# Decode attention over a KV cache on one core: VectorE and ScalarE as loops over the pairs, q's projection as a loop over 8 groups of 4 heads

## The chip, the cores and the metric

The kernel runs on one core of a Trainium2 chip. The time is the device time of one execution in microseconds. The kernel before takes 662.87 us (median of 3 runs, 662.78 to 663.01). The profiled execution has a span of 660.4 us from its first to its last instruction. In the profile PE is TensorE's matmuls, PEld its weight loads, DVE is VectorE, ACT ScalarE, POOL GpSimd and SP the engine that issues DMA transfers.

## The reference

Two blocks share one layer-normalized input x (2 tokens of width 512), and their results are added to x:

```
xn = layernorm(x)                                  # (2, 1, 512)
q  = xn @ wq          -> 2 x 32 heads of 128        # wq (512, 4096)
s  = q . k_cache * 128**-0.5                        # k_cache (2, 32, 8192, 128)
o  = softmax(s) . v_cache                           # v_cache the same shape
a  = concat(o) @ wo                                 # wo (4096, 512)
f  = relu(xn @ w1) @ w2                             # w1 (512, 1792), w2 (1792, 512)
out = x + a + f
```

All tensors are bf16. The two caches are 2 x 134 MB; everything else together is some 12 MB. The work per cache element is tiny, one product with one query.

## The kernel before, in words

There are 64 combinations of token and head. They are worked on in NP = 32 pairs; one pair of K, and one of V, is a tile of 128 partitions by 16384 elements (4 MB): 64 partitions for each of the two heads, 128 keys in each partition. R = 2 buffers hold K (ks), two hold V (vs). The second V buffer first holds wq.

What each engine does in pair t:

- TensorE (function step, L269) first waits for K(t) and for q of the pair (sQ1, L273). Then, in NG = 16 groups of 8, it transposes K blocks into PSUM (transposes, L230, matmul at L233), and two groups later multiplies the copied block with q (scores, L236, matmul at L240). Then it does the weighted sum over V of the pair before (weighted, L250, matmul at L253), and in between transposes the column of maxima (L288) and broadcasts the maximum (L291). TensorE already runs this as a loop of 16 turns of two pairs (L297), with the pair's number in a register that its waits compare with.
- VectorE and ScalarE share the copies of the transposed groups from PSUM to SBUF (kcopy, L378 to L380): groups 0, 3, 5, 8, 11 and 13 are ScalarE's (ON_ACT), the other ten VectorE's. VectorE also takes the maxima (L425, L430). ScalarE copies the broadcast maximum (nm, L483), takes Exp (L487), and copies the weighted sum of the pair before from PSUM into OTf (out_copy, L470 to L473). Both are written out in full, pair after pair: `for t in range(NP)` at L416 and L476 is a loop of the program that builds the kernel.
- GpSimd copies q of each pair into a small buffer (q2, L203), two pairs ahead.
- SyncE issues the transfers in order (L155 to L171): wq, K0, K1 and V0 at once; then for each t a K tile as soon as the transposes of pair t have ended (pT, L162), and a V tile as soon as the weighted sum that used its buffer has ended (sW, L164); last x again, w1, w2 and wo in three parts.

Semaphores order all of it. pT counts the groups of transposes over all pairs; group e of pair t is the number 16 t + e + 1, and VectorE, ScalarE and SyncE wait for such numbers. sA tells ScalarE that its own small copies are done. sO tells TensorE that a weighted sum has been copied away.

Ahead of the pairs the layer norm is done on VectorE and ScalarE, and TensorE projects q: 32 heads times 4 parts of the width, 128 products of a 128x128 block of wq with the two tokens (L216 to L225), into one PSUM tile. VectorE scales the result into qb (L408), and GpSimd copies the first two pairs' columns (L203). After the pairs come the last weighted sum, the feed-forward block, and the projections with w2 and wo (L306 to L376).

## Time and profile before

| what | number |
|---|---|
| time, median of 3 | 662.87 us |
| span of the profiled execution | 660.4 us |
| TensorE matmuls, busy | 551.0 us (83%), 12864 instructions |
| VectorE, busy | 251.4 us (38%), 433 instructions |
| ScalarE, busy | 236.7 us (36%), 389 instructions |
| read from HBM | 280.50 MB, mean 425 GB/s |
| 4 MB transfers of K | 32, median 26.8 us from issue to landing |
| 4 MB transfers of V | 32, median 31.6 us from issue to landing |
| copies L380, VectorE | 320 of 691 ns |
| copies L380, ScalarE | 192 of 1012 ns |
| products of q's projection L218 | 128, 3.6 us busy |

Busy time is the time in which an engine worked on an instruction; matmuls are pipelined, so a busy TensorE is not one at its peak. The page also cuts the span into 40 slices of 16.5 us and gives for each engine a digit, the busy share in tenths. Its DMA row is the mean busy share of the 16 DMA engines. The time from issue to landing holds the time that a transfer waits behind others in the queue. A list by waits says who waited for whom, and a list in order of time says when an instruction started and how long it took. Beside the page the trace has a record of each DMA packet, of each completion of a transfer by each of the 16 engines, and of the instructions that only the sequencers work on (register operations, branches, waits), which the page doesn't count as busy.

### The profile page before, as it was taken

Reading aid. Unit: us, or ns where it says so; the run is one execution under the profiler, and the core shown is the slowest. Engines: PE = TensorE matmul, PEld = TensorE weight load, DVE = VectorE, ACT = ScalarE, POOL = GpSimd, SP = SyncE. Lnnn points to the kernel's source line nnn. Section 1 sums busy time; section 2 is a strip of 40 time slices with the busy share of each in tenths; the row PEclk is TensorE's granted clock in tenths of the full one; section 3 lists DMA queues with packets and bytes.
Section 4 is the critical chain, followed back from the end, with each engine's and each line's share of the span. In section 5 each row is a group of like instructions: output and inputs, shape, how many; then the busy total and the mean of one; then the engine's idle time right before and its main releaser. Section 6 shows DMA issues by size and latency. Waiting matters only on the chain.

```text
span 660.4 us, 26876 instructions
## 1 busy us (share of the span) xinstructions
PE 551.0 (83%) x12864; PEld 537.0 (81%) x12864; DVE 251.4 (38%) x433; ACT 236.7 (36%) x389; POOL 8.5 (1%) x44
## 2 busy tenths in 40 slices
PE   2577999898887889788798987887997878987976
PEld 2577999888887889788798887887987878987875
DVE  1233544344343434434344443343443433443411
ACT  1242444343433334333243343333343333343410
POOL 1000000000000000000000000000000000000000
PEclk9999999998898999889899898899898989997985
DMA  9999999999999999999999999999999999999995
GB/s 381 416 438 429 424 439 427 437 427 431 437 429 437 427 431 433 429 437 429 431 435 427 439 429 431 435 427 439 427 431 433 429 439 425 435 433 429 437 417 246
DMA packets 10133, 280.73 MB, mean 425 GB/s; under 512 B 1154, under 2 KB 1156, under 8 KB 1284
## 3 DMA queue, kind: packets, MB, share of 16 engines
q1 hardware_dynamic: 10112, 280.50, 98.9%
q8 instruction: 10, 0.16, 0.1%
q14 instruction: 7, 0.06, 0.0%
q10 hardware_dynamic: 4, 0.00, 0.0%
HBM read 280.50 MB, written 0.00 MB: 425 GB/s over the span
## 4 chain that ended last, share of the span: by engine, by line
DMA 62%; PE 34%; ACT 1%; issue 1%; SPq 0%; DVE 0%
DMA ks<-in_A_k_cache_dram 56%; PE tp L233 21%; PE Sc L240 10%; DMA wo_sb<-in_A_wo_dram 5%; PE ot L253 3%; ACT kT L380 1%; PE ot L356 0%; PE Sc L288 0%; PE Sc L291 0%; SPq L171 0%; SPq L168 0%; SPq L166 0%; SPq L149 0%; SPq L167 0%; SPq L147 0%
## 5 line engine op out<-in xcount | busy, mean ns | idle before, releaser
L233 PE MATMUL tp<-identb,ks 128*128 128x128 bf16 x4096 | 324.9, 229 | 77.8 <-DMA ks<-in_A_k_cache_dram 75.9
L380 DVE COPY kT<-tp 128x1024 bf16<-128x1024 bf16 x320 | 219.7, 691 | 332.9 <-PE tp L233 332.7
L233 PEld LDWEIGHTS tp<-identb,ks 128*128 128x128 bf16 x4096 | 256.1, 103 | 81.3 <-DMA ks<-in_A_k_cache_dram 79.1
L380 ACT COPY kT<-tp 128x1024 bf16<-128x1024 bf16 x192 | 194.3, 1012 | 249.6 <-PE tp L233 249.6
L240 PE MATMUL Sc<-q,kT 128*128 128x64 bf16 x4096 | 216.3, 196 | 3.4 <-ACT kT L380 3.4
L240 PEld LDWEIGHTS Sc<-q,kT 128*128 128x128 bf16 x4096 | 178.4, 100 | 6.7 <-ACT kT L380 6.7
L253 PE MATMUL ot<-prm,vs 128*128 128x64 bf16 x4224 | 157.6, 193 | 8.5 <-issue 5.0
L253 PEld LDWEIGHTS ot<-prm,vs 128*128 128x128 bf16 x4224 | 140.5, 98 | 11.4 <-issue 8.8
L483 ACT COPY nm<-Sc 128x2 f32<-128x2 f32 x32 | 5.1, 160 | 118.2 <-PE Sc L291 118.2
L487 ACT ACTIVATE prm<-Sc,nm 64x128 bf16<-64x128 f32 x64 | 25.8, 402 | 1.4
L425 DVE TENSOR_REDUCE mcol<-Sc 64x1 bf16<-64x128 f32 x64 | 18.6, 291 | 17.6 <-PE Sc L240 17.2
L473 ACT COPY OTf<-ot 128x2 f32<-128x2 f32 x33 | 5.3, 160 | 35.3 <-PE ot L253 35.3
L430 DVE TENSOR_REDUCE mx<-Sc 1x2 bf16<-1x128 bf16 x32 | 8.9, 279 | 16.9 <-PE Sc L288 16.9
L203 POOL COPY q<-qb 128x2 bf16<-128x2 bf16 x32 | 5.8, 184 | 582.3 <-PE Sc L240 568.6
L487 ACT ACTIVATION_READ_ACCUMULATOR prm<-Sc,nm 64x1 f32 x64 | 11.8, 185 | 0.0
L218 PE MATMUL ot<-xnT,vs 128*128 128x2 bf16 x128 | 3.6, 165 | 8.3 <-DMA vs<-in_A_wq_dram 8.3
L218 PEld LDWEIGHTS ot<-xnT,vs 128*128 128x128 bf16 x128 | 3.5, 104 | 8.4 <-issue 8.4
L288 PE MATMUL Sc<-identb,mcol 128*1 128x128 bf16 x32 | 7.0, 217 | 0.0
L356 PE MATMUL ot<-OX,wo_sb 128*128 128x2 bf16 x128 | 3.7, 166 | 3.1 <-DMA wo_sb<-in_A_wo_dram 3.1
L356 PEld LDWEIGHTS ot<-OX,wo_sb 128*128 128x128 bf16 x128 | 3.6, 104 | 3.3 <-DMA wo_sb<-in_A_wo_dram 1.9
L291 PE MATMUL Sc<-mx,onesb 1*128 1x2 bf16 x32 | 5.5, 172 | 0.0
L436 DVE CAST xT<-tp 128x8 f32<-128x8 bf16 x1 | 0.2, 166 | 12.5 <-PE Sc L327 12.5
(49 smaller groups left out, 29.4 us busy)
## 6 DMA issues: line engine op xcount, KB each, us to landing
ks<-in_A_k_cache_dram SPq DMA_DIRECT2D x32, 4096.0 KB, 26.8
vs<-in_A_v_cache_dram SPq DMA_DIRECT2D x32, 4096.0 KB, 31.6
vs<-in_A_wq_dram SPq DMA_DIRECT2D x1, 4096.0 KB, 12.2
w_sb<-in_B_w_dram SPq DMA_DIRECT2D x2, 1792.0 KB, 25.9
wo_sb<-in_A_wo_dram SPq DMA_DIRECT2D x1, 2048.0 KB, 32.3
wo_sb<-in_A_wo_dram SPq DMA_DIRECT2D x1, 1536.0 KB, 35.5
wo_sb<-in_A_wo_dram SPq DMA_DIRECT2D x1, 512.0 KB, 36.3
xsb<-in_A_x_dram ACTq DMA_DIRECT2D x1, 2.0 KB
```

Source lines behind the costliest of these rows:

```text
L203: g.tensor_copy(q2[t % R][:], qb[:, 2 * t:2 * t + 2]).then_inc(sQ1, 1)
L218: i = pe.matmul(qp[:, h, :], lhsT=wq_sb[:, kt, h * Dh:(h + 1) * Dh], rhs=xnT[:, kt, :], start=(kt == 0), stop=(kt == KT - 1),)
L233: t = pe.transpose(tp[e % 4][:, i, :], ks[r][:, kk * Dh:(kk + 1) * Dh], identb[:])
L240: t = pe.matmul(Sc[r][:, 2 * kk:2 * kk + 2 * REP], lhsT=kT[e % 4][:, i, :], rhs=rep(q2[r][:]), start=True, stop=True,)
L253: t = pe.matmul(ot[r][:, 0:2 * REP], lhsT=vs[r][:, kk * Dh:(kk + 1) * Dh], rhs=rep(prm[r][:, kk, :]), start=(kk == 0), stop=(kk == KB - 1),)
L288: pe.transpose(tr_of(r), mcol[r][:], identb[:]).then_inc(sT, 1)
L291: pe.matmul(bc_of(r), lhsT=onesb[:], rhs=mx[r][:], start=True, stop=True).then_inc(sB, 1)
L356: t = pe.matmul(fin[:, c, :], lhsT=w[:, j, c * P:(c + 1) * P], rhs=act[:, j, :], start=(first and j == j0 and c == 0), stop=(last and j == ...
L380: fn(kT[e % 4][:], tp[e % 4][:]).then_inc(kR[e], 1)
L425: m = v.tensor_reduce(out=mcol[i][half, :], in_=S_of(i)[half, :, u], axis=AX.X, op=ALU.max)
L430: v.tensor_reduce(out=mx[i][:], in_=tr_of(i).rearrange("o (u m) -> o u m", u=2), axis=AX.X, op=ALU.max, negate=True,).then_inc(sX, 1)
L487: x = a.activation(out=prm[i][half, :, u], in_=S_of(i)[half, :, u], func=ACTF.Exp, bias=nm[i][half, u:u + 1], scale=1.0, accum_out=RS[half ...
```

## The change

VectorE and ScalarE get loops in the hardware's sense: 16 turns of two pairs, with the pair's number in a register, as TensorE has. A wait inside a loop can compare a semaphore with that one register, so the running number 16 t + e + 1 of pT is no longer at hand. pT becomes 16 semaphores, one per group, each counting pairs. sA, which also counted an event of the start, is replaced in the loop by a semaphore of its own, sN. In ScalarE's loop the column of RS and of OTf that a pair writes is an address worked out from the loop's number; OTf is used two columns further on, so that the copy of the sum of "pair -1" needs no case of its own. q's projection becomes a loop of 8 turns of 16 products on TensorE, with the weights' and the outputs' addresses worked out from the loop's number. The aim is a smaller program: the number of written instructions falls on all three engines. No product, copy or transfer is added or left out.

```diff
-    pT, sS, sT, sB, sW = sem("pT"), sem("sS"), sem("sT"), sem("sB"), sem("sW")
+    sS, sT, sB, sW = sem("sS"), sem("sT"), sem("sB"), sem("sW")
+    pT = [sem(f"pT{e}") for e in range(NG)]
...
-                sp.wait_ge(pT, NG * (t + 1))
+                sp.wait_ge(pT[NG - 1], t + 1)
...
-        wq_sb = vs[1][:].rearrange("p (kt n) -> p kt n", kt=KT)
-        for h in range(H):
-            for kt in range(KT):
-                i = pe.matmul(
-                    qp[:, h, :],
-                    lhsT=wq_sb[:, kt, h * Dh:(h + 1) * Dh],
-                    rhs=xnT[:, kt, :],
-                    start=(kt == 0),
-                    stop=(kt == KT - 1),
-                )
-        i.then_inc(sQ, 1)
+        HL = 4
+        with pe.Fori(0, H // HL) as hg:
+            for h in range(HL):
+                for kt in range(KT):
+                    i = pe.matmul(
+                        ot[1][:, bass.ds(hg * (HL * Bsz) + h * Bsz, Bsz)],
+                        lhsT=vs[1][:, bass.ds(hg * (HL * Dh) + (kt * H + h) * Dh, Dh)],
+                        rhs=xnT[:, kt, :],
+                        start=(kt == 0),
+                        stop=(kt == KT - 1),
+                    )
+            i.then_inc(sQ, 1)
...
-            t.then_inc(pT, 1)
+            t.then_inc(pT[e], 1)
...
-        v.wait_ge(sQ, 2)
+        v.wait_ge(sQ, 1 + H // 4)
...
-        for t in range(NP):
-            i = t % R
+        def pair(i, n):
             for e in range(NG):
                 if e not in ON_ACT:
-                    v.wait_ge(pT, NG * t + e + 1)
+                    v.wait_ge(pT[e], n)
                     kcopy(v, e)
-            v.wait_ge(sS, t + 1)
+            v.wait_ge(sS, n)
...
+        reg = nc.alloc_register(mybir.EngineType.DVE, "pairno_v")
+        v.reg_mov(reg, 0)
+        with v.Fori(0, NP // R):
+            for r in range(R):
+                v.reg_add(reg, reg, 1)
+                pair(r, reg)
...
-            out=OTn[:].rearrange("p b h -> p (b h)"), in0=OTf[:, 0:N], in1=RD[:], op=ALU.mult
+            out=OTn[:].rearrange("p b h -> p (b h)"), in0=OTf[:, 2:N + 2], in1=RD[:], op=ALU.mult
...
-        def out_copy(t):
-            c = 2 * t if t >= 0 else N
-            a.wait_ge(sW, t + 2)
-            a.copy(OTf[:, c:c + 2], ot[t % R][:, 0:2]).then_inc(sO, 1)
...
+        def out_copy(r, n, c):
+            a.wait_ge(sW, n)
+            a.copy(OTf[:, bass.ds(c, 2)], ot[r][:, 0:2]).then_inc(sO, 1)
...
+        def pair(i, n, t):
             for e in range(NG):
                 if e in ON_ACT:
-                    a.wait_ge(pT, NG * t + e + 1)
+                    a.wait_ge(pT[e], n)
                     kcopy(a, e)
-            a.wait_ge(sB, t + 1)
-            a.copy(nm[i][:], bc_of(i)).then_inc(sA, 1)
-            a.wait_ge(sA, t + 2)
+            a.wait_ge(sB, n)
+            a.copy(nm[i][:], bc_of(i)).then_inc(sN, 1)
+            a.wait_ge(sN, n)
...
-                    accum_out=RS[half, t:t + 1],
+                    accum_out=RS[half, bass.ds(t, 1)],
...
-            out_copy(t - 1)
-        out_copy(NP - 1)
+            out_copy(1 - i, n, t * 2)
+
+        a.copy(nm[0][:, 0:1], eps_t[:]).then_inc(sO, 1)
+        reg = nc.alloc_register(mybir.EngineType.Activation, "pairno_a")
+        a.reg_mov(reg, 0)
+        with a.Fori(0, NP // R) as tr:
+            for r in range(R):
+                a.reg_add(reg, reg, 1)
+                pair(r, reg, tr * R + r)
+        out_copy(1, NP + 1, N)
```

## The prediction

> **What bounds the kernel now.** I read the page first, then the waits of the DMA queue, then the order of time of the first 66 us. The page, parts 2 and 3:

> ```profile
> DMA  9999999999999999999999999999999999999995
> ...
> q1 hardware_dynamic: 10112, 280.50, 98.9%
> q8 instruction: 10, 0.16, 0.1%
> q14 instruction: 7, 0.06, 0.0%
> ```

> Every slice but the last has the 16 DMA engines at 90% or more, and the one data queue takes 98.9% of their time. In the packet records a 32 KB packet takes 1.217 us, so 16 engines give 431 GB/s, and 280.5 MB need 651 us of the 660.4 us span. The span is the queue's work plus about 2 us ahead and 5 us behind it. So a change can lose time only by letting the queue run dry, and can gain only at the ends or in what shares the DMA engines. What compute does beside a full queue costs nothing: it has slack, as the waits show.

> ```profile
> PE tp L233 <- DMA ks<-in_A_k_cache_dram: 75.9, 27, 7.4
> ```

> TensorE waits 27 times for a block of K, 75.9 us in all. K blocks land 38.9 us apart per two pairs (51.6 and 90.5 us in the completion records); TensorE, undisturbed, needs 31.8 us for two (65.0 to 96.8 us). That is 7 us of slack per turn of a two-pair loop.

> The exception is the start, where the queue is short. In order of time (start, length, engine):

> ```profile
> 13.30 3.55 PE L218 MATMUL ot<-xnT,vs 128*128 128x2 bf16 x128 [8.33 <-DMA vs<-in_A_wq_dram]
> 16.96 0.22 DVE L408 TENSOR_SCALAR qb<-ot 128x64 bf16<-128x64 f32 x1 [11.80 <-PE ot L218]
> 17.34 0.30 POOL L203 COPY q<-qb 128x2 bf16<-128x2 bf16 x2 [13.67 <-DVE qb L408]
> 24.27 2.74 PE L233 MATMUL tp<-identb,ks 128*128 128x128 bf16 x24 [7.43 <-DMA ks<-in_A_k_cache_dram]
> ...
> 36.53 0.33 SPq L144 DMA_DIRECT2D ks<-in_A_k_cache_dram  x1
> ...
> 44.48 0.33 SPq L147 DMA_DIRECT2D vs<-in_A_v_cache_dram  x1
> ...
> 57.41 0.33 SPq L144 DMA_DIRECT2D ks<-in_A_k_cache_dram  x1
> ```

> wq, K0, K1 and V0 are all that can be queued at first. By the completion records the engines end V0 between 41.9 and 43.8 us. K2 is queued at 36.53, 12.26 us after TensorE began on pair 0 at 24.27: only 5.4 us before the queue would be empty. And q, which pair 0 waits for ahead of its first transpose (the wait on sQ1), is ready at 17.6, 6.7 us before K0 lands.

> [...]
> - [...]128 weight loads and matmuls of L218 took 3.55 us, 28 ns a pair. It has no TensorE instruction whose address is in a register.
> - [...]ten 16 KB packets for TensorE, 8 KB ones for the others. They speak against trouble at branches: TensorE's loop body of some 1550 instructions[...] turned 16 times, and no block was fetched between 68.4 and 643.7 us.
> - [...]The load at 40.02 us took 1.28 us and the Exp began at 41.31[...]; I take 1.28.

> **The change part by part.**

> *VectorE and ScalarE rolled.* 433 and 389 instructions become loops of two pairs; the built program has 30 and 31 in the bodies. Added per pair: a register add, and on ScalarE three address operations, some 0.1 us each (below). VectorE is busy 38% and ScalarE 36%, and the Exp's result is wanted only half a pair later. Cost 0, hidden under the 7 us of slack.

> *A table load per turn.* The built ScalarE loop has its load of the activation table at the head of the body; before, there was one at 40.02. So 16 loads, 1.28 us each, once per two pairs. Pair 1 shows what stands there: the copy of ot ends at 44.65 and the copy of kT group 0 starts at 44.93. With a load between, the latter starts at 45.93, 1.0 us later, and behind it on TensorE stand the scores of group 0 and all that follows. So 1.0 us per two pairs, against 7 us of slack: 0 on the end.[...]

> *A semaphore per group, the copies' places in OTf shifted, sN for sA.* The same events are waited for; K's reload still waits for group 15 of the pair before. Cost 0.

> *Fewer instruction fetches.* VectorE's 8 KB blocks at 78, 259 and 452 us each held one DMA engine up by 0.9 to 1.0 us: the spread between the first and the last engine of a transfer goes from 1.87 to 2.2 to 3.2 us after the second and third, and is 3.4 us at the end. Rolled, both programs fit in what is loaded at the start. The next slowest engines lag by 2.1 us. Gain 1.3 us.

> *q's projection rolled.* This is the part with a price. The 128 products stay, in 8 turns of 16, but the weights and the outputs get register addresses. The built body has 17 register operations beside 16 products, an add and a branch. Prices:
> - A register operation on TensorE: records of 29 to 42 ns, but the next one starts 90 ns after (16.25, 16.34, 16.43 us at the head of the pairs' loop). I take 0.09; the low end is 0.035.
> - Weight load and matmul by register: not in this trace. Low end: decoded as now, 0.028 for the two.[...]
> - Turn of the loop: 0.40 (add at 64.28, branch, register operation at 64.68).

> [...]eight: 31.3 us where 3.55 stood. It begins at 13.3 and ends at 44.6. VectorE's scaling and GpSimd's copy take 0.7 more, as before (16.85 to 17.56), so pair 0 starts at 45.3 instead of 24.27. Of the added 27.7 us, 6.7 hide under the load of K0.

> What is behind it: K2's buffer is free 12.3 us after pair 0 starts, at 57.6; the first data come 1.0 us later (wq: issued 0.96, first packet 1.99), at 58.6. The queue was empty from 42.0. So 16.6 us without transfers. From there on the queue should stay filled: K3 is issued some 31 to 33 us after pair 0 starts, about 77, when V1 has until 78; K4 at about 95, when V2 has until 97. All later landings move by 16.6. The dry stretch sets all engines level again, and the lag at the end is about 2.0 instead of 3.4, which takes 1.4 off and contains the gain on fetches. Sum: +16.6 - 1.4 = +15.2, 662.9 + 15.2 = 678.1 us.

> **The rivals.**
> 1. *Register addresses are decoded as fast as fixed ones.* A turn is 1.53 + 0.45 + 0.40 = 2.4, eight 19.0; pair 0 starts at 33.0, K2's data at 46.3, dry for 4.3. 662.9 + 4.3 - 1.4 = 665.8. For it: nothing in the trace says that they are slower.[...]
> 2. *Not slower: the queue never runs dry.* Register operations cost their recorded 0.035 and overlap the array: eight turns of 1.35 make 10.8, pair 0 starts at 24.8, K2 is issued at 37.1. What is left is the gain on fetches: 661.6. For it: the 6.7 us of hiding and 5.4 us of queue. Against: the 90 ns spacing, which alone gives 12.2 us.
> 3. *Dearer still.*[...] eight turns of 5.9, pair 0 starts at 61.4, K2's data come at 74.7, dry for 33: 694.
> 4. *Loops refetch.* If VectorE's loop fetched a block at each of 16 turns, one DMA engine would lag by 16 us: some 676. TensorE's loop speaks against it; it is within the range of the forecast.

> **How the numbers follow.** Forecast 50%, rival 1 26%, rival 2 10%, rival 3 11%, rival 4 3%. Predicted 678. The range takes in rival 1 from a little below and most of the way to rival 3: 664 to 692. Slower by over 0.2%: forecast, rivals 1, 3 and 4, less a rest of rival 1, 0.87. Rival 2 is 0.2% faster, on the edge, so it is halved: faster 0.06, no change 0.07.

> **What would show it.** Right: q's matmuls in the new profile spread over about 31 us from 13.3; pair 0's transposes at about 45; the third and fourth slices of the DMA row well under 9; K2's issue at about 57. Table loads 16 or 17 at 1.28, with the kT copies of every second pair 1 us later and no more. Instruction packets of the second kind fewer than 7. Wrong: if the projection ends ahead of 25 us, the row of nines stays whole and the end moves by the fetches alone; if gaps in the DMA row come back later, it is the table load or K3's issue that I have too early.

## The result and the profile after

The changed kernel takes 669.59 us (median of 5; 669.23 to 670.04), the kernel before 662.89 beside it (662.78 to 663.06): a ratio of 1.0102, 95% interval 1.0088 to 1.0115, or 6.7 us more. It is slower, as forecast; 15.2 us were forecast.

The page of the changed kernel first: the DMA row of the 40 slices, the bytes moved in each slice, and the queues. The third slice is 33 to 50 us.

```profile
DMA  9959999999999999999999999999999999999996
GB/s 377 436 226 425 420 440 440 426 422 440 434 430 424 440 430 426 432 440 430 426 432 440 426 426 436 430 432 426 440 430 430 428 440 426 428 434 434 432 418 268
...
q1 hardware_dynamic: 10112, 280.50, 97.9%
q8 instruction: 9, 0.15, 0.1%
q14 instruction: 1, 0.01, 0.0%
```

One slice moves about half of what the others do, and no later one does. The 8 KB instruction packets are down from 7 to 1, and that one starts at 666.03, behind the last landing; the six that are gone belonged to VectorE's and ScalarE's written-out programs, and the records don't say which to which. What happened at the start, in order of time (start, length, engine, line):

```profile
13.74 2.20 PE L220 MATMUL ot<-xnT,vs 128*128 128x2 bf16 x16 [8.51 <-DMA vs<-in_A_wq_dram]
16.43 2.20 PE L220 MATMUL ot<-xnT,vs 128*128 128x2 bf16 x16 [0.48 <-issue]
...
32.20 2.20 PE L220 MATMUL ot<-xnT,vs 128*128 128x2 bf16 x16 [0.43 <-issue]
34.52 0.22 DVE L410 TENSOR_SCALAR qb<-ot 128x64 bf16<-128x64 f32 x1 [29.08 <-PE ot L220]
34.89 0.30 POOL L204 COPY q<-qb 128x2 bf16<-128x2 bf16 x2 [31.23 <-DVE qb L410]
35.22 2.72 PE L235 MATMUL tp<-identb,ks 128*128 128x128 bf16 x24 [0.82 <-POOL q L204]
...
47.91 0.33 SPq L145 DMA_DIRECT2D ks<-in_A_k_cache_dram  x1
53.03 0.33 SPq L148 DMA_DIRECT2D vs<-in_A_v_cache_dram  x1
63.86 0.33 SPq L145 DMA_DIRECT2D ks<-in_A_k_cache_dram  x1
```

The first of the eight turns of q's loop starts at 13.7, the last ends at 34.4; they come 2.63 us apart. What pair 0 waited for is now q, not K0: its release is POOL's copy. It starts at 35.22, 10.95 us later than before, and K2 is issued at 47.91, 11.4 later. Two-microsecond windows of the same stretch (window, its length, then busy time and instructions of each engine: TensorE's matmuls and loads, VectorE, ScalarE, GpSimd; the last three columns are TensorE's clock, the DMA share and GB/s, where a packet counts whole in the window in which it starts):

```profile
40.00:42.00 2.00, 2.00 (x50) 2.00 (x48) 1.01 (x2) 1.28 (x2) 0.00 (x0) 1.00 0.64 270
42.00:44.00 2.00, 2.00 (x51) 2.00 (x48) 1.30 (x3) 0.93 (x1) 0.00 (x0) 1.00 0.00 0
44.00:46.00 2.00, 2.00 (x50) 2.00 (x48) 1.30 (x3) 0.93 (x2) 0.00 (x0) 1.00 0.03 8
46.00:48.00 2.00, 2.00 (x52) 2.00 (x48) 1.30 (x3) 1.17 (x2) 0.00 (x0) 1.00 0.00 0
48.00:50.00 2.00, 2.00 (x69) 1.96 (x65) 1.20 (x3) 0.00 (x0) 0.18 (x1) 1.00 0.93 262
```

TensorE works all through it while no data are moved: V0 ended at 41.8 to 42.4, and K2 had not been asked for. K2's first packets start at 48.86, 0.95 us after its issue, and they take 1.3 to 2.3 us where the later ones take 1.21. By the completion records the first engine's part of K2 lands at 59.6 (before: 51.6), 8.0 us later, and everything after it keeps that distance to the last part of wo (first engine 660.8 against 652.8). The last engine ends wo at 662.7 against 656.2, only 6.5 later, since the spread, from the first of the 16 engines to the last, is 1.9 us instead of 3.4. So 8.0 lost and 1.5 got back; 6.7 were measured.

The rest of the run has its slack still. The waits (us in total, times, longest) and the groups concerned:

```profile
PE tp L235 <- DMA ks<-in_A_k_cache_dram: 66.0, 26, 3.4
...
PE Sc L242 <- ACT kT L382: 5.2, 16, 1.4
```

```profile
L382 ACT ACT_TABLE_LOAD x16 | 20.5, 1283 | 2.2 <-issue 0.2
```

TensorE waits for K 26 times, 66.0 us in all (before: 27 times, 75.9). The table load shows in the second line: the longest wait of the scores for ScalarE's copy is now 1.4 us, at 108 us, right behind the load at 105.78; before, the longest was 0.2 and the sum 3.4. From 200 us on the sum is 0.4 us per 100 us: TensorE waits for K there, and the load is done beside it.

### The profile page after: what moved, and what is told of

It is laid out like the page before. It is cut to its first block, busy times and chain, and to the rows that moved or that the text cites. A ratio compares the mean times of both kernels' runs of the same rounds, so it can differ in the third digit from the quotient of the medians.

```text
span 667.1 us, 27272 instructions
## 1 busy us (share of the span) xinstructions
PE 565.3 (85%) x12864; PEld 547.6 (82%) x12864; DVE 251.4 (38%) x433; ACT 256.0 (38%) x404; POOL 8.5 (1%) x44
## 3 DMA queue, kind: packets, MB, share of 16 engines
q1 hardware_dynamic: 10112, 280.50, 97.9%
HBM read 280.50 MB, written 0.00 MB: 420 GB/s over the span
## 4 chain that ended last, share of the span: by engine, by line
DMA 56%; PE 39%; ACT 2%; issue 1%; SPq 0%; DVE 0%; ACTq 0%; POOL 0%; DVEq 0%; POOLq 0%
DMA ks<-in_A_k_cache_dram 49%; PE tp L235 21%; PE Sc L242 11%; DMA wo_sb<-in_A_wo_dram 5%; PE ot L255 4%; PE ot L220 3%; DMA vs<-in_A_wq_dram 2%; ACT kT L382 2%; ACT L382 1%; PE ot L358 0%; PE Sc L290 0%; PE Sc L293 0%; SPq L172 0%; SPq L169 0%; SPq L167 0%
## 5 line engine op out<-in xcount | busy, mean ns | idle before, releaser
L220 PE MATMUL ot<-xnT,vs 128*128 128x2 bf16 x128 | 17.6, 182 | 11.6 <-DMA vs<-in_A_wq_dram 8.5
L220 PEld LDWEIGHTS ot<-xnT,vs 128*128 x128 | 13.3, 104 | 15.8 <-issue 12.0
L426 DVE TENSOR_REDUCE mcol<-Sc 64x1 bf16<-64x128 f32 x64 | 18.6, 291 | 17.6 <-PE Sc L242 17.2
L481 ACT COPY OTf<-ot 128x2 f32 (+1 forms) x33 | 5.3, 160 | 31.6 <-PE ot L255 31.6
L493 ACT ACTIVATION_READ_ACCUMULATOR prm<-Sc,nm x64 | 11.8, 184 | 0.0
## 6 DMA issues: line engine op xcount, KB each, us to landing
vs<-in_A_v_cache_dram SPq DMA_DIRECT2D x32, 4096.0 KB, 31.3
vs<-in_A_wq_dram SPq DMA_DIRECT2D x1, 4096.0 KB, 12.3
```

Source lines behind the costliest of these rows:

```text
L220: i = pe.matmul(ot[1][:, bass.ds(hg * (HL * Bsz) + h * Bsz, Bsz)], lhsT=vs[1][:, bass.ds(hg * (HL * Dh) + (kt * H + h) * Dh, Dh)], rhs=xnT ...
L426: m = v.tensor_reduce(out=mcol[i][half, :], in_=S_of(i)[half, :, u], axis=AX.X, op=ALU.max)
L481: a.copy(OTf[:, bass.ds(c, 2)], ot[r][:, 0:2]).then_inc(sO, 1)
L493: x = a.activation(out=prm[i][half, :, u], in_=S_of(i)[half, :, u], func=ACTF.Exp, bias=nm[i][half, u:u + 1], scale=1.0, accum_out=RS[half ...
```

## The experiments

The theory, Q: the loss is an empty queue. q's loop ends late, pair 0 starts late, K2 is asked for late, and each microsecond without a transfer is one at the end. The rival, L: the loops on VectorE and ScalarE cost time at every pair, with their table load, register operations and semaphores. Under it, open from the prediction: is it the register address or the register operation that makes q's loop dear? Every ratio is to the kernel before, run on the same chip. On the chips used its median was 662.76 to 662.94 us, so times of different experiments are set against each other as they are.

**q's projection written out again.**

```diff
-        with pe.Fori(0, H // HL) as hg:
-            for h in range(HL):
...
+        for h in range(H):
+            for kt in range(KT):
...
-        v.wait_ge(sQ, 1 + H // 4)
+        v.wait_ge(sQ, 2)
```

> The changed kernel with q's projection written out again as before; VectorE and ScalarE stay loops. Theory Q (the loss is the stretch in which the data queue is empty, because K2 is issued late, because q's loop ends late): the DMA row is nines from start to end, K2 is issued at about 36.5 us, and the time is 661.5 to 662.8 us: before, less up to 1.3 us for the instruction blocks that VectorE and ScalarE no longer fetch. Theory L (the loops on VectorE and ScalarE with a table load per turn cost TensorE time that reaches the end): about 669 us, as the changed kernel.

662.87 us, ratio 1.0001 (0.9993 to 1.0009). Its DMA row on the page:

```profile
DMA  9999999999999999999999999999999999999995
```

With both loops and all sixteen table loads in it, the kernel takes the time of before. That alone leaves room for a cost of the loops as large as a gain on fetches; the kernel with fixed addresses below, which has the same loops and table loads, closes it: it is faster than before by 1.5 us, just what the spread at the end lost (3.4 to 1.9). L falls. But the 1.3 us that fewer fetches were to bring don't show either; that is taken up below.

**The loop for q alone in the kernel before**, VectorE and ScalarE written out, one semaphore pT:

```diff
+        with pe.Fori(0, H // HL) as hg:
...
-        v.wait_ge(sQ, 2)
+        v.wait_ge(sQ, 1 + H // 4)
```

> The kernel before with nothing changed but q's projection, rolled as in the changed kernel. Theory Q: K2 is issued at about 47.9 us, every landing after it is 8 us later than before, and VectorE's three blocks still hold one DMA engine up by about 1 us each, so that the last engine lags by about 3.3 us where it is 1.9 in the changed kernel: 670 to 671 us. Theory L: 663 us, as before.

670.64 us, ratio 1.0116 (1.0101 to 1.0132); K2 is issued at 48.23. The whole loss comes with this one part. The interval overlaps that of the full change, so this pair of runs does not settle whether the loops on the other engines give anything back; in the records the spread at the end is 3.6 us here and 1.9 there.

**The loop for q run twice**, the same products a second time:

```diff
+        with pe.Fori(0, H // HL) as hg2:
...
-        v.wait_ge(sQ, 1 + H // 4)
+        v.wait_ge(sQ, 1 + 2 * (H // 4))
```

> The changed kernel with q's loop run twice, the second pass computing the same values again. A pass took 21 us (eight turns of 2.63). Theory Q: nothing hides any of it, since all that could hide is used up by the first pass; the queue is empty 21 us longer and the time is 669.6 + 21 = 690.6 us. Theory L: q's end still lies under slack elsewhere, so that less than half is seen: under 680 us.

690.5 us, ratio 1.0418 (1.0404 to 1.0432), 20.9 us over the changed kernel. Eight turns of 2.63 are 21.0, K2 is issued at 68.86, 20.95 later:

```profile
DMA  8930999999999999999999999999999999999996
```

Once the hiding is used up, q's loop is paid microsecond for microsecond, and the empty slices say so. The trace is that of the longest of the five runs, 691.66 us: in it K2 lands 20.8 us later than in the changed kernel, and K4, issued at 108.17 when the first engine ended V2 at 109.62, comes another 1.3 us late.

**Two turns of 64 products instead of eight of 16.**

```diff
-        HL = 4
+        HL = 16
...
-        v.wait_ge(sQ, 1 + H // 4)
+        v.wait_ge(sQ, 1 + H // 16)
```

> The changed kernel with q's loop in 2 turns of 64 products instead of 8 of 16. Each product keeps its register operation; six turns of the loop fall away, each of which left 0.48 us between the last product and the first of the next turn. Theory Q with the register operations as the main price: six times 0.48 is 2.9 us, 666.7 us. If the turns themselves were the main price, more than half of the loss of 6.7 us would go: under 666 us.

667.41 us, ratio 1.0065 (1.0051 to 1.0079).

```profile
13.89 8.74 PE L220 MATMUL ot<-xnT,vs 128*128 128x2 bf16 x64 [9.27 <-DMA vs<-in_A_wq_dram]
23.25 8.94 PE L220 MATMUL ot<-xnT,vs 128*128 128x2 bf16 x64 [0.63 <-issue]
33.02 2.72 PE L235 MATMUL tp<-identb,ks 128*128 128x128 bf16 x24 [0.82 <-POOL q L204]
```

64 products in 8.74 to 8.94 us are 137 to 140 ns each, as 2.20 / 16 = 138 before. Six turns fewer bring pair 0 forward by 2.2 us, the end by 2.2: 0.36 us a turn, where 0.48 was expected (2.9 us in all). The price stays with the products.

**Work for the empty queue:** w1 and w2 issued behind V0 instead of at the end.

```diff
             load_v(0)
+            sp.dma_start(w1_sb[:], B_w1.rearrange("(p kt) f -> p kt f", kt=KT)).then_inc(dW[0], 16)
+            sp.dma_start(w2_sb[:], B_w2.rearrange("(p j) n -> p j n", j=FT)).then_inc(dW[1], 16)
...
-            sp.dma_start(w1_sb[:], B_w1.rearrange("(p kt) f -> p kt f", kt=KT)).then_inc(dW[0], 16)
-            sp.dma_start(w2_sb[:], B_w2.rearrange("(p j) n -> p j n", j=FT)).then_inc(dW[1], 16)
```

> The changed kernel with the transfers of w1 and w2 (3.67 MB, 8.5 us at 431 GB/s) issued right behind V0 instead of near the end. They wait for nothing, so they lie in the stretch that is empty in the changed kernel (41.8 to about 49 us); q's loop, pair 0 and K2's issue stay where they are. Theory Q: the queue has no empty stretch any more, V31 lands when it did, and the work of the queue behind it is 8.5 us shorter; then TensorE, which is free for wo only some 12 us after V31 lands, sets the end: 666 to 667 us. If it were TensorE's late start itself that costs the time, and not the empty queue: 669.6 us.

667.01 us, ratio 1.006 (1.0043 to 1.0077).

```profile
DMA  9999999999999999999999999999999999999992
```

No slice is empty, and K2's first part still lands at 60.6. The bytes moved into the hole are bytes less at the end: wo has landed by 656.1, against 662.7. But the last V tile lands at 646.3 (before: 637.6), and the 19 us of TensorE's work behind it now set the end of the span (665.7). Its products with wo start without a wait, after wo has landed; before, they waited for wo twice, 3.1 us in all:

```profile
658.43 3.55 PE L358 MATMUL ot<-OX,wo_sb 128*128 128x2 bf16 x128
```

So filling the hole with other bytes returns 2.6 of 6.7 us; the rest of the loss sits in the K and V stream, which TensorE's tail waits for.

**One register address for a whole turn.** All 16 products of a turn read the same block and write the same two columns through a register. What is tried is the forecast's price of a weight load and a matmul by register address, an estimate of its author's that no trace had shown. Left out: q isn't computed (16 of its 64 columns, two per turn, get products of wq, the others are set to zero), the number of products is the same.

```diff
-                        ot[1][:, bass.ds(hg * (HL * Bsz) + h * Bsz, Bsz)],
-                        lhsT=vs[1][:, bass.ds(hg * (HL * Dh) + (kt * H + h) * Dh, Dh)],
+                        ot[1][:, bass.ds(hg * (HL * Bsz), Bsz)],
+                        lhsT=vs[1][:, bass.ds(hg * (HL * Dh), Dh)],
```

> The changed kernel in which all 16 products of a turn use the same register address for the weights and the same for the outputs, so that one register operation and an add per turn are left of 17 (q is not computed: 8 of its 64 columns get a product, the rest are zeros). It measures the step of the forecast[...]. With that price [...]the time 669.6 us. If register addresses cost nothing (28 ns for the two, as with fixed ones): 16 x 0.028 + 0.6 = 1.05 us per turn, q's loop ends at 22.2 us, ahead of K0, and the time is 661.4 to 662.9 us.

**Fixed addresses in the loop.** Left out in the same way: every turn repeats heads 0 to 3, the others are zero. No register operation stands beside a product.

```diff
+                        ot[1][:, h * Bsz:(h + 1) * Bsz],
+                        lhsT=vs[1][:, (kt * H + h) * Dh:(kt * H + h + 1) * Dh],
```

> The changed kernel with q's loop of 8 turns kept, but with fixed addresses, so that there are no register operations beside the loop's own add and branch (q is not computed: each turn repeats the first 4 heads, the other 28 are zeros). It gives the price of a turn: 16 x 0.028 + 0.45 = 0.9 us, q's loop ends at 21 us and the time is 661.4 to 662.9 us.[...]

q's stage with one register address a turn:

```profile
13.66 5.37 PE L220 MATMUL ot<-xnT,vs 128*128 128x2 bf16 x128 [8.97 <-DMA vs<-in_A_wq_dram]
22.88 2.74 PE L235 MATMUL tp<-identb,ks 128*128 128x128 bf16 x24 [3.85 <-DMA ks<-in_A_k_cache_dram]
```

and with fixed ones:

```profile
13.41 3.73 PE L220 MATMUL ot<-xnT,vs 128*128 128x2 bf16 x128 [8.53 <-DMA vs<-in_A_wq_dram]
```

Three stages of the same 128 products: 3.73 us with fixed addresses, 5.37 with one register operation per turn, 20.7 with one per product. The loads and matmuls by register address run no slower than 5.37 / 128 = 42 ns a pair with their share of the loop in it. In the records the 16 loads of the first turn start 27 ns apart on average, by register as by fixed address; the difference is between the turns, 0.2 us each, where the one register operation stands. So an address in a register is nearly free; working it out is dear. The loop itself is nearly free too: 3.73 against 3.55 us flat. Both kernels take 661.34 and 661.36 us, ratio 0.9977 in both (0.9969 to 0.9986, and 0.9968 to 0.9987): 1.5 us faster than before, the fetches' gain.

**K2 in two halves**, the first asked for after group 7 of pair 0.

```diff
+                if t == 0:
+                    sp.wait_ge(pT[NG // 2 - 1], 1)
+                    load_half(R, 0, dKh)
                 sp.wait_ge(pT[NG - 1], t + 1)
-                load_k(t + R)
+                if t == 0:
+                    load_half(R, 1, dK[0])
+                else:
+                    load_k(t + R)
```

> The changed kernel with K2 alone loaded in two halves, the first issued as soon as the first 8 groups of pair 0 are transposed (about 41.7 us instead of 47.9), the second as before. q's loop stays as it is. Theory Q: the queue is empty for about 1 us ahead of the first half and 1 to 2 us between the halves instead of 8; but then V1 ends earlier, and K3, issued at about 63.9, comes 1 to 2 us late, K4 perhaps 1 more: 4.6 to 5.4 us of loss on the first engine instead of 8, 666 to 667 us. If K3 and K4 came in time: 663.8 us. If the loss had nothing to do with K2's issue: 669.6 us.

667.04 us, ratio 1.0066 (1.0049 to 1.0082). The first half is issued at 41.83, and the first engine has all its part of K2 at 54.18, 2.6 us later than before instead of 8.0. But K3 is issued only at 64.97, when the first engine had ended V1 at 64.3: by the packet records the engines stand still for another 1.7 us at 64 to 66, and the first packets are long again. The first engine ends wo 5.6 us later than before, the spread is 1.75 us instead of 3.4, and the time is 4.2 us longer. One buffer mended shows the next: pair 1 is as late as pair 0.

**The gain that the written-out q lost.** Between the kernel with q written out (no gain) and the one with fixed addresses (1.5 us) the records differ at the end. TensorE's program comes in 16 KB packets: ten with q written out, nine with fixed addresses, two programs that differ on TensorE alone but for the wait for q and the zeros. In the former one of them starts at 649.56, and the spread over the engines goes from 2.0 us to 3.7 with the next landing; in the latter they start at 647.47 and 654.10, and it stays at 2.0. Theory P says that this block takes the gain, theory S that the written-out q costs it in some other way. To try it: fixed addresses (q not computed, as above), plus 100 products ahead of the loop whose result is thrown away, so that the program is about as long as with q written out.

```diff
+        for h in range(25):
+            for kt in range(KT):
+                pe.matmul(
+                    ot[0][:, 0:Bsz],
...
```

> The kernel with fixed addresses in q's loop (q is not computed, as there), plus 100 further products, written out ahead of the loop and thrown away, so that TensorE's program ahead of the pairs is about as long as with q written out. The added 2.8 us lie in the idle time before K0 lands, so the queue stays full and K2 is issued at about 36 us. Theory P (the gain of 1.5 us depends on where TensorE's own 16 KB blocks fall at the end, as the records of the two kernels suggest): the block near the end is fetched at about 650 us again and hits a lagging engine, the spread at the end is about 3.5 us, the time about 662.8. Theory S (the written-out q costs 1.5 us in some way of its own, or the loop gives it): the spread stays at 2.0 and the time at 661.4.

662.52 us, ratio 0.9995 (0.9987 to 1.0003). The block starts at 652.11, and the spread goes from 1.96 us at the landing at 647.8 to 3.48 at the next. 1.2 of the 1.5 us are gone, though this interval and that of the fixed addresses touch at 0.9987. P holds as far as these records go: the size of the program ahead of the pairs, not q itself, moves a block to where it costs the gain. What decides on which engine a block falls isn't settled: with one register address a block at 649.20 left the spread at 2.1.

**Five turns of the loop and the rest written out.** All is computed.

```diff
-        HL = 4
-        with pe.Fori(0, H // HL) as hg:
+        HL, HR = 4, 20
+        with pe.Fori(0, HR // HL) as hg:
...
+        for h in range(HR, H):
+            for kt in range(KT):
...
-        v.wait_ge(sQ, 1 + H // 4)
+        v.wait_ge(sQ, 7)
```

> The changed kernel with heads 0 to 19 in five turns of the loop and heads 20 to 31 written out; all is computed. Theory Q: five turns of 2.63 us plus 48 products of 28 ns are 14.5 us and end at about 28.2, pair 0 begins at about 29, K2 is issued at about 41.5, just as the queue runs dry (41.8 to 42.4): 0 to 1.5 us without transfers, less what the fetches give (up to 1.5): 661.5 to 663.5 us. Were the loss not from an empty queue but from the loop as such, five eighths of 6.7 us would be left: 667.

663.7 us, ratio 1.0019 (1.001 to 1.0027).

```profile
26.57 1.43 PE L231 MATMUL ot<-xnT,vs 128*128 128x2 bf16 x48
28.82 2.72 PE L246 MATMUL tp<-identb,ks 128*128 128x128 bf16 x24 [0.82 <-POOL q L204]
```

```profile
40.93 0.33 SPq L145 DMA_DIRECT2D ks<-in_A_k_cache_dram  x1
46.04 0.33 SPq L148 DMA_DIRECT2D vs<-in_A_v_cache_dram  x1
60.82 0.33 SPq L145 DMA_DIRECT2D ks<-in_A_k_cache_dram  x1
```

The times of the start are as worked out, and so is 1.0 us at K2. The forecast's upper end is missed by 0.2 because a second stretch was left out of it: K3 is issued 1.45 us before V1's first part lands (62.27) and itself lands 0.9 us late. Before, those 1.45 us were 3.9. In the packet records K3's first packets follow V1's with next to no gap, but most of them take 1.5 to 2.4 us instead of 1.21. So, as an estimate from lead plus delay, a transfer must be asked for some 2 us ahead of the end of the queue (0.8 + 1.0 at K2, 1.45 + 0.9 at K3), not just ahead of it. The last landing has a spread of 2.85 us here, after a block at 655.47.

**Three turns of the loop and the rest written out**, the same with HR = 12 (and a wait for 5):

> The changed kernel with heads 0 to 11 in three turns of the loop and heads 12 to 31 written out; all is computed. Theory Q: three turns of 2.63 us and 80 products of 28 ns end at about 23.8 us, pair 0 begins at about 24.5 and K2 is issued at about 36.8, both as in the kernel before: no dry stretch. What is left is the fetches: [...]I expect the block near the end at about 651 us, still before the last part of wo has landed. If it hits a lagging engine again: spread 3.5, time 662.8. If it comes late enough or hits another: spread 2.0, time 661.4, and this is faster than both kernels.

663.02 us, ratio 1.0 (0.9992 to 1.0008).

```profile
19.00 2.20 PE L220 MATMUL ot<-xnT,vs 128*128 128x2 bf16 x16 [0.43 <-issue]
21.26 2.29 PE L231 MATMUL ot<-xnT,vs 128*128 128x2 bf16 x80
24.37 2.72 PE L246 MATMUL tp<-identb,ks 128*128 128x128 bf16 x24 [0.82 <-POOL q L204]
```

Pair 0 starts at 24.37 against 24.27 before, and K2 is issued at 36.29. Three turns, 7.9 us of the dear loop, cost nothing: they fit under the load of K0. The block near the end came at 649.89 and lifted the spread from 1.95 to 3.3, which takes the gain again. So no kernel that computes all of q was measurably faster than the one before.

## Why the prediction was right in its direction and wrong in its size

Step by step, as the prediction has them:

- **The bound.** Right. The queue sets the end, and time was lost where it ran dry: the run with q twice adds 20.9 us for 20.95 of later issue.
- **VectorE and ScalarE rolled, the semaphores per group, at nothing.** Right: 1.0001 with them alone, and 0.9977 with q's loop at fixed addresses beside them.
- **A table load per turn, 1.0 us later, hidden.** Right. 16 loads of 1.28 us; one makes TensorE wait 1.4 us at 108, the later ones fall where it waits for K, 66 us in all.
- **The price of a register operation, 0.09 us.** Right: 0.096 from one product's register operation to the load behind it, in the sequencer's records. The operation itself is recorded with 46 to 79 ns; what fills the rest isn't shown.
- **Weight load and matmul by register. This is the step that failed.** They take 28 ns for the two, as with fixed addresses; in the records load and matmul follow the register operation 7 ns apart, and the next register operation 21 ns later. The dearer price in the forecast was the author's estimate, which nothing in the trace before showed. With 28 ns for the two, as rival 1 had it, eight turns are 19.0 us where the forecast had 31.3: 12.3 us were not there.
- **The turn, 3.91 us (31.3 / 8).** It is 2.63: 16 x (0.096 + 0.028) = 1.98, 0.18 for the longer steps in a turn (at a new head 157 instead of 124 ns), and 0.47 for the way to the next turn. Eight turns ended at 34.4, not at 44.6.
- **From pair 0 to K2's issue, 12.3 us.** Right: 12.7 (35.22 to 47.91).
- **From issue to the first data, 1.0 us.** Right for the first packet, 0.95 us, but too short for the stream: the first packets take 1.3 to 2.3 us. K2's first engine lands at 59.59; eight packets of 1.217 us each before that put a start at full rate at 49.85, 1.94 us after the issue. The record of wq in the kernel before has such packets too, of up to 2.3 us, right behind the first packet at 1.99 from which the prediction took its 1.0. The part loop gives about 1.8 at K2 and 2.4 at K3, worked out as lead plus delay. With it goes why rival 1's 665.8 was low by 3.8: pair 0 at 35.2 instead of 33.0 is 2.2 (turns of 2.63 instead of 2.4, and a start at 13.7), the way to the issue 0.4, the restart 0.9; 0.3 is left over.
- **The dry stretch, 16.6 us.** It was 8.0 (41.8 to 49.85, the last 1.0 of it in the long first packets): the failed price took 12.3 off, the longer turns (2.2), the way to the issue (0.4), the restart (0.9) and V0's end at 41.8 instead of 42.0 put 3.7 back.
- **No second dry stretch.** Right for this kernel: K3 was issued at 63.86, 5.4 us ahead of V1's end at 69.3. It is no rule: with K2 in halves, and with five turns, K3 was late, and with q twice K4.
- **The lag at the end 2.0 instead of 3.4.** The number is right, 1.9, and 1.5 us back; the reason given is not. The dry stretch was to set all engines level. But with q's loop alone the stretch is as dry and the lag at the end is 3.6, and with fixed addresses nothing is dry and the lag is 1.9. What takes the 1.5 us off is that VectorE and ScalarE fetch no blocks on the way, which the prediction had priced at 1.3 and then counted as contained. It holds here since TensorE's blocks at 656.37 and 660.28 left the spread at 1.9. As a gain in general it fails: with q written out, TensorE's own block gave it back.

Sum as measured: 8.0 - 1.5 = 6.5 us; the run shows 6.7. Rivals 2, 3 and 4 did not occur: the queue did run dry; the loads were not dearer; and no block was fetched per turn: one 8 KB packet came in the whole span, at its end. That agrees with what the prediction read from the packet records of TensorE's loop, with no block between 68.4 and 643.7 us.

## What to carry to other kernels

Where a queue of transfers sets the time, find the stretch in which it is short, and add up in that stretch the chain from the instruction you lengthen to the next transfer's issue; 17 us added to q's stage cost 8.0 at the queue, the next 21 cost 20.9. Rolling this flat sequence of short TensorE instructions into turns of 16 products was nearly free with fixed addresses (0.02 us a turn) and with one shared by a turn (0.2 us more); one address worked out per product made each 138 ns instead of 28. A transfer that is to keep a queue full had to be issued some 2 us before the queue ended (estimate from the leads and delays above).

## What the runs showed of the hardware

| kernel | TensorE's 16 KB packets near the end, start | spread ahead | spread at the end | time |
|---|---|---|---|---|
| before | 643.69, 652.03, 656.11 | 3.3 | 3.4 | 662.8 to 662.9 |
| q written out | 642.07, 649.56, 656.37 | 2.0 | 3.5 | 662.87 |
| fixed, padded | 643.82, 652.11, 656.35 | 2.0 | 3.5 | 662.52 |
| three turns | 642.83, 649.89, 656.79 | 2.0 | 3.3 | 663.02 |
| fixed addresses | 641.06, 647.47, 654.10 | 2.0 | 1.9 | 661.36 |
| one address | 642.28, 649.20, 654.36 | 2.1 | 2.2 | 661.34 |
| two turns | 650.46, 656.91, 661.58 | 2.0 | 2.2 | 667.41 |
| five turns | 641.99, 648.39, 655.47 | 1.8 | 2.85 | 663.70 |

In the first four, each with ten such blocks, the ninth hits an engine that is already behind (in the kernel before it raises one from 2.1 to 3.3, beside one that was at 3.3 already, so it costs nothing there). With fixed addresses and with one address there are nine blocks, and none raises the spread by more than 0.1. The number doesn't decide it: two turns has ten blocks and ends at 2.2, five turns has nine and ends at 2.85.
